# A delta-rule and SwiGLU kernel: new costs, overlaps and tile-shape changes in the planner that writes its order

## The chip, the cores and the metric

The kernel runs on one core of one Trainium2 chip. The metric is the device time in microseconds: the median of three timed runs before the change is 740.26 us (738.58 to 741.01). The engines are called here as the profile calls them: PE is TensorE (PEld its weight loads), DVE is VectorE, ACT is ScalarE, POOL is GpSimd and SP is SyncE, which issues most DMAs.

## The reference

Two blocks follow each other. The first is a delta-rule attention over 768 steps, for 4 batches and 8 heads of size 48. The second is a SwiGLU feed-forward over the 3072 tokens (model 384, hidden 1536), behind an RMS norm.

```python
k_n = k / (norm(k) + 1e-6)
for t in range(S):
    y[:, :, t] = einsum('bhd,bhde->bhe', q[:, :, t], state)
    v_old = einsum('bhde,bhd->bhe', state, k_n[:, :, t])
    state = state + beta_t * einsum('bhd,bhe->bhde', k_n[:, :, t], v[:, :, t] - v_old)
x = y.transpose(0, 2, 1, 3).reshape(B * S, H * D)
xn = x / sqrt(mean(x * x) + 1e-6) * rms_g
out = (silu(xn @ w_gate) * (xn @ w_val)) @ w_out
```

## The kernel before

The 768 steps are cut into 12 chunks of 64. Inside a chunk the recurrence becomes matrix algebra for all 32 heads of the batch at once. For each chunk the kernel does these things:

- `norms` and `prep` normalize the keys, transpose them (`turn`, L489), multiply them with each other (`scores`, L512), send the products through DRAM into another layout, and solve a triangular system on DVE. The solve is a chain of 15 planned steps, each one a product (L673) and a reduction (L679). Two merges on PE (L754 and L776) put the halves of the inverse together.
- `qpart` does the transposes and scores of the queries.
- `recur` applies the state to keys and queries (`on_state`, L815), the inverse to the corrected values (L857), the masked scores to the result (L871), and updates the state (L980). It then normalizes the rows, transposes them (L948) and forms seven sums of the feed-forward's input (L966).
- `ffn` does the feed-forward of the chunk: 30 products on PE (L1116, eight matmuls each), which DVE (L1126) or ACT (L1128) takes out of PSUM, a Silu on ACT (L1132) and a product on DVE (L1133). Then `down` (L1172, L1181) does seven products with the output weights. Both are bilinear schemes that use fewer products and more sums. Chunks 0 and 1 use `ffn_plain` (L1023, L1005) instead.

The matmuls have three kinds of tile. Most use the whole array (128 rows by 128 columns). The groups at L512, L815, L857, L871 and L980 are made of 64 small matmuls of 64 rows by 64 columns. The merges use 128 rows by 32 columns, and two early transposes (L730) 32 by 32. In steady state there are seven groups of 64 rows and two merges per chunk.

The weights come as 64-bit words (two halves of a double). Eighteen tiles are converted by a chain of four DVE operations each (L408, L414, L419, L424); for the first nine the two parts are added on PE (L439 and L440).

The order of all instructions on all engines is not written by hand. `Plan.add` records each group of instructions as an operation with an engine, a duration in microseconds, its inputs and outputs, the PSUM banks that it takes and gives back, and a first priority. `Plan.run` then plans 60 times and keeps the plan with the earliest end. `forward` simulates the engines: each time it picks, among all operations whose inputs are known, the one with the earliest start, and among equal starts the one with the smallest key. `backward` goes through the plan from its end and gives each operation the latest start that it could have as its new key. Between rounds the keys are shaken a little. The best order is then emitted, and each engine works through its part of it strictly in order. Up to 70 us filler matmuls (L1262) are put into planned gaps of PE, one per 0.2 us of gap.

The durations come from constants and four linear formulas, for instance `V = lambda n: 0.13 + 0.0011 * n` for a DVE operation over n elements and `A = lambda n: 0.2 + 0.0008 * n` for ACT. A planned result is available on another engine after `op.lat` (0.15 us, 0.7 for a DMA) plus a slack (0 to 1 us by part of the program). On its own engine it is available at once.

## Time and profile before

| | |
|---|---|
| median of 3 runs | 740.26 us (738.58 to 741.01) |
| the profiled execution's own time | 739.21 us |
| its span, first to last instruction | 737.5 us |
| mean granted PE clock | 0.996 |
| PE busy | 719.1 us (97%), 10238 matmuls |
| DVE busy | 575.0 us (78%), 1144 instructions |
| ACT busy | 308.5 us (42%) |
| POOL busy | 151.2 us (20%) |
| DMA | 54.68 MB, mean 74 GB/s |

Busy time is the time in which an engine had an instruction in work. A busy PE is not PE at its peak, since matmuls are pipelined: one of 128 columns lasts 0.277 us in the records, and the next starts 0.112 us after it. To see what PE loses between two groups, one compares the starts of the groups in the timeline, not their lengths. In a timeline line the first number is the start in us, the second the length, then come engine, line, operation, output and inputs, tile shape, size and count; brackets hold the idle time before it and what ended that. In the table of stretches each line has the stretch, its length, and then the busy time of PE, PEld, DVE, ACT and POOL with the count of instructions, the granted clock, the DMA share and GB/s.

### The profile page before, as it was taken

The numbers are of one execution on the slowest core, as the hardware profiler recorded it, in microseconds if no ns is written. First come the engines' busy times: TensorE is split into PE (matmuls) and PEld (weight loads), VectorE is DVE, ScalarE is ACT, GpSimd is POOL, SyncE is SP. The second block draws the span as 40 slices with busy tenths as digits, with TensorE's granted clock in tenths as the row PEclk, the third lists the DMA queues.
The fourth block names the chain that finished last, engine by engine and source line by source line (L and its number), as shares of the span: only waits on it lengthen the run. The fifth ranks groups of instructions, "written<-read, shape, count | busy, mean of one in ns | idle before, by whom it ended". The sixth has DMA issues, their size and how long they took to land. (4 is left out here: it accounts for less than half of the span.)

```text
span 737.5 us, 23665 instructions
## 1 busy us (share of the span) xinstructions
PE 719.1 (97%) x10238; PEld 660.1 (90%) x10238; DVE 575.0 (78%) x1144; ACT 308.5 (42%) x691; POOL 151.2 (20%) x153
## 2 busy tenths in 40 slices
PE   9999998999999999999999999999999999899997
PEld 9877766877889999999999999999999999898997
DVE  4999989789997966876967856977976876877362
ACT  4535636122335336345345355345246245244241
POOL 4100303322312111413203203203031311200000
PEclk9999999999999999999999999999999999999999
DMA  7848677331350142253152162234143123040000
GB/s 162 222 74 250 151 171 203 74 57 33 67 106 16 31 81 58 45 99 61 32 107 46 24 112 49 45 66 72 34 81 72 24 51 67 3 67 7 22 2 21
DMA packets 206999, 54.68 MB, mean 74 GB/s; under 512 B 199216, under 2 KB 202288, under 8 KB 206896
## 3 DMA queue, kind: packets, MB, share of 16 engines
q1 hardware_dynamic: 201552, 52.19, 34.3%
q10 hardware_dynamic: 5344, 0.98, 0.8%
q8 instruction: 80, 1.31, 0.7%
q14 instruction: 23, 0.19, 0.1%
HBM read 40.83 MB, written 12.32 MB: 72 GB/s over the span
## 5 line engine op out<-in xcount | busy, mean ns | idle before, releaser
L1126 DVE TENSOR_TENSOR tmp<-tmp,bank 128x512 f32<-128x512 f32 x180 | 122.2, 684 | 83.4 <-PE bank L1116 67.6
L1116 PE MATMUL bank<-xf,w_in 128*128 128x128 f32 x1440 | 181.3, 277 | 0.0
L1116 PEld LDWEIGHTS bank<-xf,w_in 128*128 128x128 f32 x1440 | 169.6, 192 | 3.5 <-issue 1.4
L1116 PE MATMUL bank<-xf,more 128*128 128x128 f32 x960 | 124.2, 277 | 0.5 <-DVE tmp L1126 0.4
L1116 PEld LDWEIGHTS bank<-xf,more 128*128 128x128 f32 x960 | 114.9, 192 | 2.4 <-DVE tmp L1126 0.8
L1128 ACT COPY tmp<-bank 128x512 f32<-128x512 f32 x120 | 68.4, 587 | 76.9 <-PE bank L1116 71.1
L679 DVE TENSOR_REDUCE acc<-acc 128x30 f32<-128x90 f32 (+4 forms) x180 | 85.1, 473 | 6.2
L1132 ACT ACTIVATE tmp<-tmp 128x256 f32<-128x256 f32 x120 | 49.9, 417 | 76.2 <-DVE tmp L1126 75.8
L673 DVE TENSOR_TENSOR acc<-acc,at 128x60 f32<-128x60 f32 (+4 forms) x180 | 65.2, 362 | 5.0 <-POOL at L656 1.2
L1133 DVE TENSOR_TENSOR hf<-tmp 128x256 f32<-128x256 f32 x120 | 57.4, 488 | 14.0 <-ACT tmp L1132 13.0
L1172 PE MATMUL bank<-wo_sb,hf 128*128 128x192 f32 x360 | 64.3, 328 | 1.1 <-DVE hf L1133 1.1
L1172 PEld LDWEIGHTS bank<-wo_sb,hf 128*128 128x128 f32 x360 | 58.1, 190 | 1.7 <-DVE hf L1133 1.3
L532 POOL TENSOR_TENSOR knrm<-ksum,half 128x16 f32<-128x16 f32 x12 | 36.7, 3060 | 105.0 <-DVE ksum L531 105.0
L626 POOL TENSOR_TENSOR at<-at,beta_b 128x1024 f32<-128x1024 f32 x10 | 24.0, 2397 | 161.4 <-DMA at<-dkk 161.4
L1262 PE MATMUL bank<-ident 128*128 128x128 f32 x310 | 38.8, 285 | 1.4 <-POOL ident masks.py:199 1.4
L1262 PEld LDWEIGHTS bank<-ident 128*128 128x128 f32 x310 | 37.3, 200 | 2.1 <-POOL ident masks.py:199 1.4
L700 POOL COPY acc<-acc 128x128 f32<-128x128 f32 x40 | 16.2, 437 | 105.4 <-DVE acc L679 104.7
L1023 PE MATMUL bank<-xp,w_in 128*128 128x256 f32 x144 | 35.0, 396 | 0.0
L1005 PE MATMUL bank<-wo_sb,hf 128*128 128x384 f32 x96 | 34.4, 491 | 0.1
L1023 PE MATMUL bank<-xf,w_in 128*128 128x256 f32 x144 | 33.6, 383 | 0.2 <-ACT xf L951 0.2
L1023 PEld LDWEIGHTS bank<-xp,w_in 128*128 128x128 f32 x144 | 28.0, 198 | 5.0
L1023 PEld LDWEIGHTS bank<-xf,w_in 128*128 128x128 f32 x144 | 26.8, 190 | 5.0 <-ACT xf L951 0.3
(172 smaller groups left out, 1079.4 us busy)
## 6 DMA issues: line engine op xcount, KB each, us to landing
at<-dkk SPq DMA_DIRECT2D x23, 256.0 KB, 4.0
more<-in_moe_w_gate_dram SPq DMA_DIRECT2D x6, 768.0 KB, 7.0
q<-in_q_dram SPq DMA_DIRECT2D x24, 192.0 KB, 4.4
more<-in_moe_w_val_dram SPq DMA_DIRECT2D x6, 768.0 KB, 7.9
vt<-in_v_dram SPq DMA_DIRECT2D x24, 192.0 KB, 3.7
more<-in_moe_w_out_dram SPq DMA_DIRECT2D x6, 768.0 KB, 5.9
out_dram<-tmp SPq DMA_DIRECT2D x48, 96.0 KB, 2.2
k<-in_k_dram SPq DMA_DIRECT2D x23, 192.0 KB, 4.1
```

Source lines behind the costliest of these rows:

```text
L532: P.add("POOL", 2.95, lambda: nc.gpsimd.tensor_tensor(out=knrm[i2], in0=ksum[i2], in1=half, op=ALU.pow), pn, r=[("ksum", i2), "half"], w=[ ...
L673: nc.vector.tensor_tensor(out=acc[:, 1:3, 0:n, j + 2 : W].rearrange("p a i t -> p i a t"), in0=acc[:, old, 0:n, j : j + 2, None].to_broadc ...
L679: nc.vector.tensor_reduce(out=acc[:, new, 0:n, j + 2 : W], in_=acc[:, lo : lo + 3, 0:n, j + 2 : W].rearrange("p a i t -> p i t a"), axis=A ...
L1005: nc.tensor.matmul(po[p].t[:, 0:DM], hf[:, spot(f), 128 * p : 128 * p + 128], wo_sb[:, spot(f)], start=(f == f0), stop=(f == f1 - 1), skip ...
L1023: nc.tensor.matmul(ps.t[:, TOK * side : TOK * side + TOK], w_in[:, side, h_, 3 * t + i_, n : n + 128], x_[:, 2 * t : 2 * t + 2].rearrange( ...
L1116: nc.tensor.matmul(g.t[:, 128 * z : 128 * z + 128], fac[:, side, 128 * f : 128 * f + 128], xf[:, xs], start=(begin and z == 0), stop=False ...
L1126: P.add("DVE", V(512), lambda t=t, g=g: nc.vector.tensor_tensor(out=t, in0=t, in1=g.t, op=ALU.add), -1, r=[g], w=[tk], last=g)
L1128: P.add("ACT", A(512), lambda t=t, g=g: nc.scalar.copy(t, g.t), -1, r=[g], w=[tk], last=g)
L1132: P.add("ACT", A(256), lambda t=t: nc.scalar.activation(out=t[:, 0:256], in_=t[:, 0:256], func=ACTF.Silu), -1, w=[tk])
L1133: P.add("DVE", V(256), lambda t=t, f0=f0, p=p: nc.vector.tensor_tensor(out=hf[:, spot(f0) : spot(f0) + 2, 128 * p : 128 * p + 128], in0=t[ ...
L1172: nc.tensor.matmul(g.t[:, 0:192], a_[:, f], b_[:, f], start=(begin and f == 0), stop=(f == 5), skip_group_check=True)
L1262: nc.tensor.matmul(warm[:, 0:128], ident, ident)
```

## The change

Only the planner's costs change; the operations themselves, their data and their banks stay as they are. There are four parts.

1. Overlap. `OVERLAP` lets an engine start its next operation 0.08 us (DVE), 0.1 us (ACT) or 0.06 us (POOL) before the last one ends, whether or not the next one uses the last one's result. The backward pass does the same.
2. Hops. `Op.hop` replaces the constant 0.15 us between engines: 0.2 us behind PE, 0.15 us from another engine to PE, 0.05 us between the others. DMAs keep their 0.7 us.
3. Tile shape. Each PE operation carries a `mode`: 64 for the groups of 64 rows, 32 for the two merges, 128 for all others (the early transposes at L730 and the small product at L593 too). When the mode differs from that of the last PE operation, the forward pass adds 0.1 us. In the choice among operations with equal start, the key of an operation whose mode differs is made worse by `STICK`, 2 us.
4. Durations. Groups of 64 rows, transposes, merges and a few others get shorter durations.

```diff
+OVERLAP = {"PE": 0.0, "ACT": 0.1, "DVE": 0.08, "POOL": 0.06, "SP": 0.0}
+STICK = 2.0
...
+    def hop(self, user):
+        return self.lat if self.dma else 0.2 if self.eng == "PE" else 0.15 if user.eng == "PE" else 0.05
...
+        op.mode = self.rows if eng == "PE" else None
...
-                    if best is None or (s, op.key, op.n) < best[0]:
-                        best = ((s, op.key, op.n), op)
+                    key = op.key + (STICK if op.mode is not None and op.mode != mode else 0.0)
+                    if best is None or (s, key, op.n) < best[0]:
+                        best = ((s, key, op.n), op)
...
-            end = at[op.eng] = s + op.dur
+            if op.mode is not None and op.mode != mode:
+                s += 0.1
+                op.start, mode = s, op.mode
+            end = s + op.dur
+            at[op.eng] = end - min(OVERLAP[op.eng], op.dur)
...
-                u.at = max(u.at, end + (0.0 if u.eng == op.eng and not op.dma else op.lat + u.slack))
+                u.at = max(u.at, at[op.eng] if u.eng == op.eng and not op.dma else end + op.hop(u) + u.slack)
...
-            op.key = front[op.eng] = t - op.dur
+            op.key = t - op.dur
+            front[op.eng] = op.key + min(OVERLAP[op.eng], op.dur)
...
-                gap = d.end - d.start - d.dur + (0.0 if d.eng == op.eng and not d.dma else d.lat + op.slack)
+                gap = d.end - d.start - d.dur + (0.0 if d.eng == op.eng and not d.dma else d.hop(op) + op.slack)
...
-                    P.add("PE", 1.5, s6, pr, r=cvk + [("cvw", n), "ident"], w=[("cvp", n, x_)], ps=ps)
+                    P.add("PE", 1.35, s6, pr, r=cvk + [("cvw", n), "ident"], w=[("cvp", n, x_)], ps=ps)
...
-            P.add("PE", 0.55, tr, pr, r=r + ["ident"], w=[ps, keys[hv]], ps=ps)
+            P.add("PE", 0.44, tr, pr, r=r + ["ident"], w=[ps, keys[hv]], ps=ps)
...
-        P.add("PE", 1.16, sc, pr, r=r, w=ps + w, ps=ps)
+        P.rows = 64
+        P.add("PE", 0.99, sc, pr, r=r, w=ps + w, ps=ps)
+        P.rows = 128
```

The other durations change in the same way, with `P.rows` around those of small tiles: merge L754 from 0.7 to 0.5 and L776 from 1.1 to 0.9 (rows 32), `on_state` from 1.1 to 0.98, L857 and L871 from 0.6 to 0.49 for each half, L980 from 1.2 to 0.98 (rows 64), the transposes at L948 from 0.45 to 0.34, the Square on ACT of chunk 0 from `A(192) + 0.2` to `A(192) + 0.15`, and `down`'s products from 1.96 to 1.95.

## The prediction, made before the changed kernel was run

> **What bounds the kernel now.** I read the page's span and busy lines first, then busy time by stretch, then TensorE's timeline.
>
> ```profile
> span 737.5 us, 23665 instructions
> ...
> PE 719.1 (97%) x10238; PEld 660.1 (90%) x10238; DVE 575.0 (78%) x1144; ACT 308.5 (42%) x691; POOL 151.2 (20%) x153
> ```
>
> TensorE has work at hand for 719.1 of 737.5 us; 18.4 us are idle. The stretches (length, then PE, PEld, DVE, ACT, POOL busy, clock, DMA) say where:
>
> ```profile
> 80.00:105.00 25.00, 23.34 (x375) 18.43 (x374) 23.85 (x45) 10.40 (x25) 4.57 (x2) 1.00 0.54 121
> 105.00:130.00 25.00, 22.62 (x526) 17.54 (x523) 22.59 (x35) 15.68 (x30) 7.13 (x4) 0.96 0.79 209
> ...
> 346.00:401.00 55.00, 53.48 (x840) 51.18 (x839) 41.83 (x92) 23.85 (x56) 13.13 (x13) 1.00 0.35 62
> ...
> 621.00:673.00 52.00, 49.47 (x753) 47.39 (x751) 39.86 (x83) 18.97 (x44) 9.35 (x11) 1.00 0.18 33
> ...
> 700.00:737.50 37.50, 32.86 (x254) 32.27 (x252) 18.17 (x35) 9.98 (x23) 0.00 (x0) 0.97 0.05 11
> ```
>
> Up to 105 us VectorE is nearly full (18.5, 18.8, 19.1 of 20 us in the stretches of 20 to 80 us, 23.85 of 25 here): the start is VectorE's, and TensorE idles 2.5 us there (0 to 80) besides fillers. From 80 to 130 it idles 1.66 + 2.38 us, from 130 to 700 the stretches add up to 7.25 us, and 4.64 us lie behind 700. So a new order can win TensorE's waits, an earlier start, or the work that TensorE does twice: changes of its tile shape. TensorE's timeline shows these (start, length, shape, count):
>
> ```profile
> 267.34 1.95 PE L1116 MATMUL bank<-xf,more 128*128 128x128 f32 x16
> 269.13 0.60 PE L489 MATMUL bank<-ident,k 128*128 128x128 f32 x4
> 269.57 1.06 PE L1116 MATMUL bank<-xf,more 128*128 128x128 f32 x8
> ...
> 407.36 1.16 PE L1116 MATMUL bank<-xf,more 128*128 128x128 f32 x8
> 408.36 1.06 PE L1116 MATMUL bank<-xf,w_in 128*128 128x128 f32 x8
> 409.34 1.15 PE L871 MATMUL bank<-u,pt 64*64 64x48 f32 x64
> 410.31 1.15 PE L512 MATMUL bank<-qt,kt 64*64 64x64 f32 x64
> 411.39 2.22 PE L1172 MATMUL bank<-wo_sb,hf 128*128 128x192 f32 x12
> ```
>
> Sixteen matmuls between other 128-row work take 269.13 - 267.34 = 1.79 us; between two 64-row groups they take 409.34 - 407.36 = 1.98, 0.19 more. A 64-row group followed by another takes 410.31 - 409.34 = 0.97; followed by 128 rows, 411.39 - 410.31 = 1.08, 0.11 more. An excursion to 64 rows and back therefore costs 0.19 + 0.11 = 0.30 us. Counting shapes along TensorE's records: 183 changes, 65 excursions to 64 rows (some 84 planned groups, so about 20 already share one), 27 to 32 columns or rows. All excursions cost about 92 x 0.30 = 28 us.
>
> **The change, part by part.** No instruction but TensorE's filler matmuls (one per 0.2 us of planned idle before 70 us; 310 now) changes in number and no byte moves; the queues of SP, ScalarE and POOL hold the same issues, in an order that the planner writes anew. Costs are constants of the planner, so each edit acts only through the order.
>
> *Tile rows (mode, +0.1 us, STICK 2.0).* Among operations that can start at the same time a 64-row group now joins the last one if its key is up to 2 us later, and a 64-row group is put off until it is 2 us more urgent than 128-row work. That needs equal start times, which a full TensorE gives. Reading before's order by hand: some 10 pairs of 64-row groups stand within 2 us of each other with neither feeding the other (114 to 119 us, 213 and 216, 294 and 297, 426 and 428, 461 to 465, 569 to 571, 574 to 576), and some 17 within 4 us, which delaying the first and advancing the second spans. Chain members (the groups at L857, then L871 and L980, which need its result copied) cannot join. Bounds: none merges, 0; every chunk from 180 us on has three excursions instead of five or six, 30 fewer, -9 us. I take 15 at 0.30: **-4.5 us**, nearest to the 17 pairs. Delaying a 64-row group by 2 us delays what queues behind it on ScalarE or VectorE (the copy of u, r, the state); the recurrence of a chunk takes some 10 to 25 us of a 55 us period (L857 begins at 402.2 and 453.8 us), so I cost it at nothing; without that slack it costs 2 us a chunk.
>
> *Durations.* A transpose group drops from 0.55 to 0.44, x transposes 0.45 to 0.34, 64-row groups 1.1 to 1.2 down to 0.98 plus the change. The timeline has 0.97 and 4 transposes in 0.44 (269.13 to 269.57). Over a steady chunk the transposes, 64-row groups and merges were planned at 4 x 0.55 + 2 x 0.45 + 2 x 1.16 + 2 x 1.1 + 3 x 1.2 + 0.7 + 1.1 = 13.0 us and become 12.2 with 5.3 excursions at 0.2 and the merges' own; by the rows above they take 12.8, since an excursion costs 0.30. The 30 products, 0.9 planned, take 0.89. So the plan was about 0.5 us a chunk too long and becomes about 0.4 too short. Nothing moves by itself: 0.
>
> *Hops.* All were 0.15; now 0.2 behind TensorE, 0.15 into it, 0.05 otherwise.
>
> ```profile
> 719.84 1.05 PE L1116 MATMUL bank<-xf,w_in 128*128 128x128 f32 x8
> ...
> 720.93 0.69 DVE L1126 TENSOR_TENSOR tmp<-tmp,bank 128x512 f32<-128x512 f32 x1 [1.21 <-PE bank L1116]
> 721.65 0.42 ACT L1132 ACTIVATE tmp<-tmp 128x256 f32<-128x256 f32 x1 [1.30 <-DVE tmp L1126]
> ```
>
> Planned end 719.84 + 0.9 = 720.74, next start 720.93: 0.19. VectorE to ScalarE: 721.65 - 721.62 = 0.03. So hops become right; where they were long, VectorE merely idled in the plan.
>
> *Overlaps.* VectorE's next operation may now start 0.08 before the last ends, whatever they are. Rows that carry the doubt (VectorE and TensorE, 637 to 643 us):
>
> ```profile
> 637.21 0.35 DVE L673 TENSOR_TENSOR acc<-acc,at 128x192 f32<-128x192 f32 x1
> 637.59 0.48 DVE L679 TENSOR_REDUCE acc<-acc 128x96 f32<-128x288 f32 x1
> ...
> 641.23 0.42 DVE L673 TENSOR_TENSOR acc<-acc,at 128x256 f32<-128x256 f32 x1
> ...
> 642.20 0.34 DVE L1181 TENSOR_TENSOR tmp<-tmp,bank 128x192 f32<-128x192 f32 x1
> ...
> 642.59 2.22 PE L1172 MATMUL bank<-wsum,hf 128*128 128x192 f32 x12 [1.45 <-DVE tmp L1181]
> ```
>
> Inside a step of the triangular solve the second instruction starts 0.03 after the first (637.59 against 637.21 + 0.35). Four steps take 641.23 - 637.21 = 4.02 us; by 0.36 + 0.0052 n m with n m of 96, 110, 120, 126 the old plan had 3.79, the new one, less 4 x 0.08, has 3.47. The short price grows from 0.06 to 0.14 us a step. Five such steps stand before L1181, and TensorE waits 1.45 us for it. Independent neighbours do overlap: over VectorE's records the gap behind an eviction is -0.08, so 18 evictions and 12 products (L1133) a chunk were each planned that much too long and become right. The old plan's errors cancelled in part; the new one keeps the short ones alone.
>
> [...]
>
> For the 7.25 us of waits between 130 and 700: lower bound all go, -7.25; upper bound, the 105 steps that follow directly on another are each 0.08 later and TensorE waits for all of it, +8.4. VectorE is idle a fifth of the time, which takes up most lateness, and the evictions' price gets better while the steps' gets worse: I take **+0.5**, nearest to no change.
>
> *80 to 130 us.* 1.94 us idle before 127.0 is followed by 24 matmuls in 7.0 us that take 0.216 x 24 = 5.2 elsewhere (clock 0.96 in that stretch). A new order need not repeat this pair: bounds -5.9 (4.04 idle and 1.85 of clock) and +4 (another such pair); I take **-1.0**, since the pair is one accident of the order; where it goes, VectorE, busy 22.6 to 23.9 of 25 us here, is late next.
>
> *Before 80 us.* VectorE is the limit and its work is unchanged. Weight conversion chains four dependent operations, each planned 0.08 short where the records have +0.03: 0.46 per tile, nine tiles, 4.1 us late against the plan at worst; at best TensorE's 2.5 idle goes. I take 0. The tail (4.64 us) is the last sums and stores: 0, at most 0.7 either way.
>
> Sum: -4.5 + 0.5 - 1.0 = -5.0 against the profiled execution's 739.21 us (737.5 of span and 1.7 around it): 734.2. That run lies 1.05 below the median 740.26, so the median should be about **735**.
>
> **Rivals.**
> *Slower, by the chained steps.* The solve's steps, planned 0.14 short, push VectorE behind and TensorE waits at L1181 and at evictions. For: the 1.45 us wait stands exactly there. Against: VectorE is idle a fifth of the time. Price: +8.4, with only five merges -1.5: 739.2 + 6.9 + 1.05 = 747. It decides once more than two thirds of 8.4 us reach TensorE (5.5 us, what the forecast gains).
> *Much faster.* Excursions fall to three a chunk (-9) and half the waits go (-3.6): 740.3 - 12.6 = 728. For: TensorE is full, so every tie counts. Against: the chain of a chunk keeps its groups apart.
> *No effect on the order that matters.* Merges stay few and waits swap places: 739 to 741. For: 20 groups share an excursion already.
>
> **How the numbers follow.** Forecast 38%, slower 28%, much faster 17%, no effect 17%. The measurement tells 0.3% (2.2 us) from no change. Faster: nearly all of the forecast, all of "much faster" and a little of "no effect", 0.55; same 0.19; slower 0.26. The range runs from 724 (both large gains and some of the start) to 748; the forecast alone spans 731 to 739.
>
> **What would show it.** Right: about 50 excursions to 64 rows instead of 65, in pairs taking 0.97 each; PE busy shortfall from 130 to 700 us near 7; the clock at 1.00 in 105 to 130. Wrong: long waits of L1172 or L1116 for VectorE behind runs of L673 and L679; first L1023 matmul (81.7 us now) later; unchanged excursions.

## The result, and the profile after

The changed kernel is slower: 748.50 us median (748.47 to 750.48, 4 runs) beside 739.42 (736.16 to 741.01, 4 runs) for the kernel before on the same chip, a ratio of 1.0135 [1.0095, 1.0175]. (A ratio, here and below, compares all runs of two kernels, with its 95% interval in brackets; it is not the quotient of the two medians.) Its profiled execution took 750.48 us. The forecast was 735, so sign and size are wrong, and the time lies just above the upper end of the range, 748. Times are medians; one execution of a later experiment, 755.84 us at a clock of 0.989, was disturbed and is left out of its median.

The page of the changed kernel, span and busy time by engine:

```profile
span 748.8 us, 23665 instructions
...
PE 723.8 (97%) x10264; PEld 667.4 (89%) x10264; DVE 557.3 (74%) x1144; ACT 310.5 (41%) x691; POOL 150.3 (20%) x153
```

The work is the same but for 26 more filler matmuls (10264 against 10238). Line numbers move by 17 to 33 in the code of the phases: the products are now L1149, their evictions L1159, `down` L1205 and L1214, the scores L529, `on_state` L838, the key transposes L506, `ffn_plain` L1056, the solve L692 and L698. Its stretches (length, then busy time of PE, PEld, DVE, ACT, POOL, clock, DMA):

```profile
80.00:105.00 25.00, 25.00 (x321) 19.12 (x323) 22.82 (x41) 15.23 (x32) 4.76 (x2) 1.00 0.71 152
105.00:130.00 25.00, 22.16 (x574) 16.73 (x567) 22.27 (x36) 11.48 (x23) 5.04 (x4) 1.00 0.92 233
130.00:200.00 70.00, 65.41 (x564) 51.02 (x557) 63.42 (x110) 18.29 (x42) 20.69 (x17) 0.95 0.23 39
200.00:346.00 146.00, 143.11 (x2158) 132.80 (x2157) 105.42 (x230) 62.46 (x143) 35.73 (x38) 1.00 0.39 72
346.00:401.00 55.00, 53.23 (x844) 51.66 (x845) 39.16 (x89) 25.30 (x57) 12.87 (x13) 1.00 0.35 62
401.00:621.00 220.00, 217.50 (x3433) 211.08 (x3435) 165.04 (x365) 100.07 (x229) 53.41 (x52) 0.99 0.32 58
...
700.00:748.80 48.80, 44.15 (x346) 43.55 (x344) 22.16 (x40) 13.27 (x29) 0.00 (x0) 0.99 0.07 17
```

From 130 to 700 us TensorE now idles 4.59 + 2.89 + 1.77 + 2.50 = 11.75 us (the two stretches left out are full), where it idled 7.25, and 130 to 200 has a clock of 0.95. The tail is as it was (4.65 idle against 4.64).

Stretches at equal times hide what is late, so the traces were also read for the time at which TensorE had done an equal share of its matmuls (each weighted by its row's start-to-start time, fillers left out). Against before, the changed kernel is 6.6 us late at 6% of the work (88.8 against 82.3 us), 9.4 at 12% (138.9 against 129.5), up to 18.3 in between (at 70%), and 11.3 at the end. In the tables below, "start" is the time to 12% and "rest" the time from there to the last matmul: before 129.5 and 603.5, after 138.9 and 605.4. Most of the loss is the start, and the rest gained nothing. Each start and rest is that of one execution, and these two stem from a series in which the kernel before had a median of 739.42 us, beside 734.49 to 736.12 in the later ones, so 2 or 3 us between rows of different series say little.

**The shape changes went as priced.** Changes of tile shape along TensorE fall from 183 to 158, excursions to 64 rows from 65 to 54. A merged pair, from the timeline of the changed kernel:

```profile
408.47 1.15 PE L1011 MATMUL bank<-u,k 64*64 64x48 f32 x64
409.44 1.11 PE L898 MATMUL bank<-u,pt 64*64 64x48 f32 x64
410.48 2.94 PE L1149 MATMUL bank<-xf,w_in 128*128 128x128 f32 x24
```

The first of the pair takes 0.97 to the next start, the second 1.04. At half of the prediction's 0.30 for each change, 25 fewer are worth 3.75 us; this is an estimate, and no run measures it by itself.

**The start is late from the first instruction.** VectorE's first instructions, before:

```profile
0.86 0.07 DVE L349 MEMSET half<- 128x16 f32 x1 [0.86 <-PEq L1280]
...
1.00 0.55 DVE L335 MEMSET k<- 128x256 f32 x2
```

and after:

```profile
7.62 0.95 DVE L548 TENSOR_REDUCE ksum<-r 128x16 f32<-128x768 f32 x1 [7.62 <-ACT r L547]
...
8.82 0.27 DVE L352 MEMSET k<- 128x256 f32 x1
```

The padding of the first keys is written behind a reduction that waits 7.62 us for a DMA and a Square. TensorE's first key transposes need that padding, and more fillers stand before them as well (70 instead of 42). Before:

```profile
1.41 6.71 PE L1262 MATMUL bank<-ident 128*128 128x128 f32 x42 [1.41 <-POOL ident masks.py:199]
7.96 1.04 PE L489 MATMUL bank<-ident,k 128*128 128x128 f32 x8
```

and after:

```profile
1.42 10.75 PE L1295 MATMUL bank<-ident 128*128 128x128 f32 x70 [1.42 <-POOL ident masks.py:199]
12.00 1.04 PE L506 MATMUL bank<-ident,k 128*128 128x128 f32 x8
```

They start at 12.00 us instead of 7.96, the solve's first scaling (L645) at 32.36 instead of 27.95 behind 2.37 us of waiting for a DMA, and the first feed-forward matmul at 85.91 instead of 81.72. In this plan the 4 us do not come back.

**TensorE stalls inside groups, and the profile names no releaser.** TensorE's waits from 130 us on ("issue" is a wait behind which nothing shows; in us in total, times, longest), the longest ones before:

```profile
PE bank L1172 <- DVE tmp L1181: 2.9, 3, 1.5
PE bank L512 <- issue: 1.1, 2, 0.7
...
PE bank L815 <- issue: 0.5, 1, 0.5
```

and after:

```profile
PE bank L838 <- issue: 4.6, 2, 3.0
PE bank L529 <- issue: 3.1, 2, 1.7
PE bank L884 <- issue: 1.5, 1, 1.5
PE bank L1149 <- DVE tmp L1159: 1.4, 2, 1.0
...
PE bank L1205 <- DVE tmp L1214: 0.4, 1, 0.4
```

Waits for VectorE fell from 5.8 to 2.1 us, but waits for nothing rose from 1.6 to 9.2. All but one of these (1.5 us in front of a single group, L884 at 186.04 us) lie in the middle of 64-row groups that follow each other, as here in TensorE's timeline:

```profile
124.75 1.03 PE L529 MATMUL bank<-qt,kt 64*64 64x64 f32 x52
128.08 0.39 PE L529 MATMUL bank<-qt,kt 64*64 64x64 f32 x11 [2.30 <-issue]
...
129.24 0.93 PE L838 MATMUL bank<-state,kt 64*64 64x48 f32 x49
133.18 0.57 PE L838 MATMUL bank<-state,kt 64*64 64x48 f32 x12 [3.02 <-issue]
...
135.15 1.85 PE L506 MATMUL bank<-ident,q 128*128 128x128 f32 x8
```

Three groups lose 5.3 us, and eight transposes behind them take 1.85 us that take 1.04 at 12.00: the trace records a granted clock of 0.50 from 133.34 us on, for 3.41 us.

So there were three suspects: how the planner chooses (the start), what the merged groups run into (the stalls), and the price of chained steps, which the prediction had named as the danger.

### The profile page after: what moved, and what is told of

The parts are those of the page before. It is cut to its first block, busy times and chain, and to the rows that moved or that the text cites. A ratio compares the mean times of both kernels' runs of the same rounds, so it can differ in the third digit from the quotient of the medians.

```text
span 748.8 us, 23665 instructions
## 1 busy us (share of the span) xinstructions
PE 723.8 (97%) x10264; PEld 667.4 (89%) x10264; DVE 557.3 (74%) x1144; ACT 310.5 (41%) x691; POOL 150.3 (20%) x153
## 3 DMA queue, kind: packets, MB, share of 16 engines
q8 instruction: 80, 1.31, 0.8%
## 4 chain that ended last, share of the span: by engine, by line
PE 77%; DVE 13%; issue 3%; SPq 3%; DMA 2%; ACT 1%; POOL 1%; DVEq 0%; POOLq 0%; ACTq 0%
PE bank L1149 30%; PE bank L1205 17%; PE bank L1056 8%; PE bank L1038 3%; DVE acc L698 3%; PE bank L529 3%; SPq L340 3%; DVE acc L692 3%; PE bank L838 2%; PE bank L506 2%; PE bank L1295 2%; DVE tmp L1159 2%; DMA at<-dkk 2%; PE bank L884 1%; PE bank L797 1%
## 5 line engine op out<-in xcount | busy, mean ns | idle before, releaser
L1149 PE MATMUL bank<-xf,w_in 128*128 128x128 f32 x1440 | 182.7, 278 | 0.2
L1159 DVE TENSOR_TENSOR tmp<-tmp,bank 128x512 f32<-128x512 f32 x180 | 120.7, 681 | 73.9 <-PE bank L1149 69.7
L1149 PEld LDWEIGHTS bank<-xf,w_in 128*128 128x128 f32 x1440 | 170.8, 192 | 3.1 <-DVE tmp L1159 0.6
L1149 PE MATMUL bank<-xf,more 128*128 128x128 f32 x960 | 125.1, 277 | 1.4 <-DVE tmp L1159 1.4
L1149 PEld LDWEIGHTS bank<-xf,more 128*128 128x128 f32 x960 | 115.7, 192 | 3.8 <-DVE tmp L1159 2.0
L698 DVE TENSOR_REDUCE acc<-acc 128x30 f32<-128x90 f32 (+4 forms) x180 | 85.1, 473 | 6.2
L692 DVE TENSOR_TENSOR acc<-acc,at 128x60 f32<-128x60 f32 (+4 forms) x180 | 63.4, 352 | 3.3
L1205 PE MATMUL bank<-wo_sb,hf 128*128 128x192 f32 x360 | 63.7, 327 | 0.3 <-DVE xp L1198 0.3
L1205 PEld LDWEIGHTS bank<-wo_sb,hf 128*128 128x128 f32 x360 | 58.2, 190 | 0.6 <-ACT kk L626 0.4
L645 POOL TENSOR_TENSOR at<-at,beta_b 128x1024 f32<-128x1024 f32 x10 | 23.8, 2384 | 173.0 <-DMA at<-dkk 132.9
L1166 DVE TENSOR_TENSOR hf<-tmp 128x256 f32<-128x256 f32 x120 | 52.7, 452 | 7.5 <-ACT tmp L1165 6.9
L1214 DVE TENSOR_TENSOR tmp<-tmp,bank 128x192 f32<-128x192 f32 x30 | 10.6, 353 | 46.5 <-PE bank L1205 39.6
L1295 PE MATMUL bank<-ident 128*128 128x128 f32 x336 | 42.4, 288 | 1.4 <-POOL ident masks.py:199 1.4
L1295 PEld LDWEIGHTS bank<-ident 128*128 128x128 f32 x336 | 41.0, 203 | 2.2 <-POOL ident masks.py:199 1.4
L1038 PE MATMUL bank<-wo_sb,hf 128*128 128x384 f32 x96 | 36.5, 511 | 0.0
L1056 PE MATMUL bank<-xf,w_in 128*128 128x256 f32 x144 | 34.3, 384 | 0.0
L1056 PE MATMUL bank<-xp,w_in 128*128 128x256 f32 x144 | 32.9, 380 | 0.1
L719 POOL COPY acc<-acc 128x128 f32<-128x128 f32 x40 | 19.9, 528 | 64.6 <-DVE acc L698 64.3
L1056 PEld LDWEIGHTS bank<-xp,w_in 128*128 128x128 f32 x144 | 27.0, 190 | 5.4 <-ACT qt L518 0.4
```

The lines of the kernel that those rows point to most:

```text
L692: nc.vector.tensor_tensor(out=acc[:, 1:3, 0:n, j + 2 : W].rearrange("p a i t -> p i a t"), in0=acc[:, old, 0:n, j : j + 2, None].to_broadc ...
L698: nc.vector.tensor_reduce(out=acc[:, new, 0:n, j + 2 : W], in_=acc[:, lo : lo + 3, 0:n, j + 2 : W].rearrange("p a i t -> p i t a"), axis=A ...
L1038: nc.tensor.matmul(po[p].t[:, 0:DM], hf[:, spot(f), 128 * p : 128 * p + 128], wo_sb[:, spot(f)], start=(f == f0), stop=(f == f1 - 1), skip ...
L1056: nc.tensor.matmul(ps.t[:, TOK * side : TOK * side + TOK], w_in[:, side, h_, 3 * t + i_, n : n + 128], x_[:, 2 * t : 2 * t + 2].rearrange( ...
L1149: nc.tensor.matmul(g.t[:, 128 * z : 128 * z + 128], fac[:, side, 128 * f : 128 * f + 128], xf[:, xs], start=(begin and z == 0), stop=False ...
L1159: P.add("DVE", V(512), lambda t=t, g=g: nc.vector.tensor_tensor(out=t, in0=t, in1=g.t, op=ALU.add), -1, r=[g], w=[tk], last=g)
```

## The experiments

All ratios are against the kernel before on the same chip. "Seed" is the seed with which the planner shakes its due times: another seed gives another order by the same rules, and so shows how much one plan's luck is worth.

### A probe of TensorE's instruction supply

This is a small program of its own, with runs of 1, 1, 2, 3, 4 and 6 groups of 64 small matmuls (48 columns), six groups with 192 columns, and one more, parted by 80 matmuls of the whole array. The series runs twice, the second time beside loads of 192 KB. These loads end at 182 us, and the program's own store of 4.6 MB follows them until 194 us: so the second run of four stands beside the store, and the second run of six beside nothing.

> This kernel leaves the whole computation out: it runs groups of 64 small TensorE matmuls (64 by 64 tiles) in runs of 1, 1, 2, 3, 4, 6 groups between stretches of 128-row matmuls, once more 6 groups with 192 instead of 48 moving columns, then 1; first with no other transfers, then the whole series again beside 48 loads of 192 KB. Theory 'instruction supply': a 64-row group holds 128 instructions in 0.97 us, and TensorE's own instruction transfers of 16 KB (256 instructions) cannot follow two or three groups in a row. Then runs of 1 pass at 0.97 to 1.08 us, runs of 4 and 6 with 48 columns show gaps of 1 us or more inside a group that the profile puts down to nothing it shows, the run of 6 with 192 columns (same number of instructions, several times longer) shows none, and the gaps grow in the second series. Rival 'tile shape': the gaps come with every group of 64 rows, and also with 192 columns. Rival 'something of the kernel' (PSUM banks, data not shown): no gaps here at all.

TensorE's timeline, the quiet series (runs of 3, 4 and 6, and the 192 columns):

```profile
51.38 3.01 PE L39 MATMUL ps<-mov,ident 64*64 64x48 f32 x192
...
63.45 3.35 PE L39 MATMUL ps<-mov,ident 64*64 64x48 f32 x211
67.99 0.90 PE L39 MATMUL ps<-mov,ident 64*64 64x48 f32 x45 [1.19 <-issue]
...
83.63 2.07 PE L39 MATMUL ps<-mov,ident 64*64 64x48 f32 x125 [1.63 <-issue]
...
96.05 15.83 PE L39 MATMUL ps<-mov,ident 64*64 64x192 f32 x384
```

and the second series (the run of 3 beside the loads, that of 4 beside the store, and the end of that of 6):

```profile
172.12 0.32 PE L39 MATMUL ps<-mov,ident 64*64 64x48 f32 x5 [1.96 <-issue]
...
188.58 2.59 PE L39 MATMUL ps<-mov,ident 64*64 64x48 f32 x85 [4.33 <-issue]
191.10 10.88 PE L31 MATMUL warm<-ident 128*128 128x128 f32 x80
...
210.14 0.79 PE L39 MATMUL ps<-mov,ident 64*64 64x48 f32 x37 [1.65 <-issue]
210.86 10.83 PE L31 MATMUL warm<-ident 128*128 128x128 f32 x80
```

Nothing in this program depends on another engine, and three groups in a row run without a stall in quiet; four lose 1.19 us. Beside the loads three lose 1.96 us, and beside the store four lose 4.33, after which 80 matmuls take 10.88 us instead of the 9.20 that they take between the other runs. The form with 192 columns has the same tiles and as many instructions, takes 15.83 us for six groups in both series, 2.7 times as long as six at 0.97, and shows no stall. So in these runs neither the tile shape nor the number of instructions makes the stalls, but how fast the instructions follow each other: 128 in 0.97 us against 128 in 2.64. The page's queue "q8 instruction" moves 80 packets with 1.31 MB in the kernel, 16 KB each, while TensorE has 2 x 10264 instructions (a matmul and its weight load each): 257 instructions a packet. Their number goes with TensorE's instructions: 35 packets in the probe with its 4492 matmuls, 81 in e3_port_chain with 10334. By this count, an estimate, two 64-row groups need a packet in 1.94 us. While the quiet run of six stalled, the packets started at 81.21, 84.72 and 88.47 us, one in 3.5 to 3.8. So the author's reading is that the instructions run short there; why shorter runs pass is not shown. How much of the longer stalls of the second series is due to the transfers is not shown either: the runs also fall on other places in a packet there.

The kernel's own stalls stand beside these packets in time. In the 20 traces (the probe's among them) TensorE has 71 waits of over 0.4 us behind which nothing shows, from 20 us on; 69 of them end 1.2 to 1.75 us after a packet has landed, while the packets come 8.9 us apart on average. In the changed kernel packets land at 126.43 and 131.74 us, and the two stalls shown above end at 128.08 and 133.18. In the kernel before one lands at 125.47, and the idle 1.94 us end at 127.01. The two exceptions are L884 in the changed kernel (1.50 us) and a merge in the run with `STICK = 0.0` (1.28 us). A wait that ends so behind a packet is called an instruction stall below.

### The port edit: how the start got lost

The planner holds that DVE and POOL share a port (no run tests that), and lets one use it only after the other's end. The change lets POOL itself come free 0.06 us before its end, but holds the port until the end. POOL's next memset could then always start 0.06 us before VectorE's, and the earliest start wins whatever the urgency. Before, both starts were equal, and the key decided.

```diff
             if op.port:
-                held[op.eng] = end
+                held[op.eng] = at[op.eng]
```

> The changed kernel, but in the planner the port that VectorE and GpSimd share is given back 0.06 or 0.08 us before an operation's end, as the engine itself is. Theory 'port': GpSimd's overlap of 0.06 lets its next memset always start before VectorE may, so VectorE's memsets of the keys' padding are planned behind all six of GpSimd's, at 5.3 us, the first transposes are planned at 7.1 instead of 4.3 us, and 28 more filler matmuls hold TensorE until 12.0 us instead of 8.0. Here the first transposes begin at 8 us and the time falls by 4, to 744. Rival 'the start is paid elsewhere': the transposes begin at 8 us, but the first feed-forward matmul still begins 3 us or more later than in the kernel before, because the plan counts chained VectorE operations too short: 747 to 749.

Measured: 735.36 us, ratio 0.9995 [0.9973, 1.0016]. TensorE's first key transposes, behind 44 fillers instead of 70:

```profile
9.32 1.04 PE L506 MATMUL bank<-ident,k 128*128 128x128 f32 x8
```

The transposes start at 9.32 instead of 12.00, the first feed-forward matmul at 77.73 instead of 85.91, and the start takes 128.0 us. So the rival, by which that first matmul still comes 3 us late, falls. With one line of the planner changed, this plan has lost nothing against the kernel before. It also has 5.2 us of instruction stalls instead of 12.2, and no half clock instead of 10.24 us of it; how much of the gain is the port is taken up below, with the other seeds.

### Taking the overlap or the preference away

```diff
-OVERLAP = {"PE": 0.0, "ACT": 0.1, "DVE": 0.08, "POOL": 0.06, "SP": 0.0}
+OVERLAP = {"PE": 0.0, "ACT": 0.0, "DVE": 0.0, "POOL": 0.0, "SP": 0.0}
```

> The changed kernel with all overlaps set to 0; durations, hops and the price of tile shapes stay. Theory 'overlaps': the loss of 11 us comes from VectorE being planned too short, at the start and after. Then the first feed-forward matmul begins within 1 us of the kernel before (81.7 us), and with the shape changes saved the time is 735 to 738. Rival 'instruction supply' alone: the start is mended (-6), but adjacent groups of 64 rows still stall TensorE by some 14 us against 5 before: 741 to 744. Rival 'luck of the plan': 745 to 750.

Measured: 744.92 us, ratio 1.0102 [1.0053, 1.0151]. The transposes come at 8.46 us, so the overlap is what unbalanced the port; but the start is still 132.7 us and the rest 607.1. The sign of the theory, a first feed-forward matmul within 1 us of 81.7, is missed: it comes at 86.86. The overlap alone is not the whole loss. This plan has 6.7 us of instruction stalls and 6.83 us of half clock, against 4.0 and 3.41 in the kernel before.

```diff
-STICK = 2.0
+STICK = 0.0
```

> The changed kernel with STICK 0: a change of tile shape still costs 0.1 us in the plan, but nothing is put off to join groups of 64 rows. Theory 'instruction supply': adjacent groups become few again, TensorE's waits put down to nothing the profile shows fall from 14 to 5 us or less, the clock stays full, and against 3 us of shape changes that come back the time falls by 5 to 8, to 741 to 744. Rival 'the merges are a gain': the time rises by 3, to 752. The start stays as late as in the changed kernel in both.

Measured: 744.77 us, ratio 1.0125 [1.0075, 1.0174]. Shape changes go up to 193 and stalls without a releaser after 130 us go down to 1.6 us. Start 131.2 (expected as late as with the preference, 138.9), rest 606.9. Without the preference the rest is within 1.5 us of the change with it: about 35 more changes cost 5.2 us, and 3.8 us fewer waits (8.2 against 12.0) give most of it back. In this planner the preference bought nothing: what it saves in shape changes it pays in instruction stalls.

### Other seeds: how much is luck

```diff
-        rng = random.Random(1)
+        rng = random.Random(2)
```

(or 3), for the change as it is, for the change with the port edit, and for the kernel before.

> The changed kernel with another start of the planner's random shaking (2 instead of 1), to see how much of a time is the luck of one plan. Theory 'port': the memsets are again planned behind GpSimd's, the first key transposes begin at 11 us or later, and the time is 744 to 752. Rival 'luck of the plan': the time may land anywhere from 733 to 752, and the pair with the port mended overlaps with it.

> The same with start 3. Theory 'port': 744 to 752, first key transposes at 11 us or later. Rival 'luck of the plan': anywhere from 733 to 752. Theory 'instruction supply': its waits on nothing the profile shows grow with the number of places where three 64-row groups stand in a row (7 planned here, 8 in the changed kernel, 4 with start 2).

> The port mended as in e1_port, start 2. Theory 'port': first key transposes before 9.5 us, 733 to 739. Rival 'luck of the plan': e1_port was a lucky plan, and this one lies at 740 to 750. Theory 'instruction supply': this plan has seven runs of three and two of five 64-row groups, more than the changed kernel, so the waits on nothing shown are 10 us or more and the time is at the upper end, 738 or above.

> The port mended, start 3. Theory 'port': first key transposes before 9.5 us, 733 to 739. Rival 'luck of the plan': 740 to 750. Theory 'instruction supply': three runs of three groups and one of five, so 4 to 6 us of such waits.

> The kernel before with another start of the planner's shaking (2). It tells how much of the gap of 5 us that is left between the changed kernel with the port mended (735, 744, 743) and the kernel before is the luck of the old plan. Theory 'the rest is luck': 738 to 746. Rival 'the rest is the new costs' (overlaps for chained operations): 733 to 738.

> The same with start 3. Theory 'the rest is luck': 738 to 746; rival 'the rest is the new costs': 733 to 738. This plan has two runs of four 64-row groups and two of three, so theory 'instruction supply' expects 4 to 8 us of waits on nothing shown.

| planner | seed | ratio | start | rest | waits after 130 us: for DVE, for nothing shown | instruction stalls from 20 us on, time at half clock before the program's last 12 us |
|---|---|---|---|---|---|---|
| before | 1 | 1 | 129.5 | 603.5 | 5.8, 1.6 | 4.0, 3.41 |
| before | 2 | 0.9954 [0.9935, 0.9973] | 126.8 | 600.5 | 3.5, 0.6 | 3.4, 0 |
| before | 3 | 1.0013 [0.9989, 1.0036] | 123.0 | 605.1 | 7.6, 1.2 | 1.3, 3.41 |
| after | 1 | 1.0135 [1.0095, 1.0175] | 138.9 | 605.4 | 2.1, 9.2 | 12.2, 10.24 |
| after | 2 | 1.0133 [1.0095, 1.0171] | 132.8 | 608.1 | 7.2, 2.7 | 5.9, 3.41 |
| after | 3 | 1.0185 [1.0152, 1.0217] | 135.9 | 607.6 | 8.1, 3.3 | 5.7, 6.83 |
| port edit | 1 | 0.9995 [0.9973, 1.0016] | 128.0 | 603.2 | 4.5, 4.6 | 5.2, 0 |
| port edit | 2 | 1.0109 [1.0077, 1.0140] | 130.5 | 606.2 | 8.4, 1.7 | 2.9, 6.83 |
| port edit | 3 | 1.0110 [1.0065, 1.0155] | 127.2 | 608.2 | 12.1, 1.4 | 2.3, 0 |

The loss of the change is no luck: its three plans average 1.0151, those of before 0.9989. The whole recovery of e1_port was partly luck: its three average 1.0071. So the plans with the port edit have 0.8% of the 1.6% less, nearly all in the start (135.9 to 128.6 on average, the rest 607.0 to 605.9).

That is not all the port's. In all three seeds the transposes come 2.5 to 2.7 us earlier with the edit (9.32, 8.91 and 9.12 against 12.00, 11.39 and 11.80), and 6% of TensorE's work is done some 2.8 us earlier on average, about half of the 5.8 us by which the change is behind the kernel before there. The first feed-forward matmul shows it less clearly: 85.91, 80.98 and 82.84 in the change, 81.72, 80.75 and 79.72 before. But the plans with the edit have fewer instruction stalls too. Stalls and half of the time at half clock, an estimate of what both cost, come to 11.3 us a plan in the change, 4.6 with the edit and 4.0 before. This difference, 6.7 us, is as large as the whole recovery, and no run tells whether the edit or chance makes it. By this estimate stalls and clock are some 7 of the 12 us that the change loses.

The 9.2 us of stalls belong to one plan, but the two others wait for VectorE in their place, and the waits of all three are 11 to 12.5 us together with ScalarE's, against 4.1 to 8.8 before. With the port edit TensorE still waits 4.5 to 12.1 us for VectorE. So another cause lies in the rest.

The length of the runs alone does not foretell the stalls. Counted from the planned runs of three groups and more, 10 us or more of waits for nothing shown were expected with the port edit and seed 2, 4 to 6 with seed 3, and 4 to 8 in the kernel before with seed 3. They were 1.7, 1.4 and 1.2.

### Chained steps at their own price

In the records of the kernel before, the product and reduction of a solve step, of which the second uses the first's result, stand 0.03 us apart in all 180 places, while the median gap of VectorE behind an eviction (L1126) is -0.08 us (130 places where the next instruction follows within 0.2 us). The change's forward pass gives both the second price. (Its backward pass does not: there only operations that do not use each other's result overlap, since `gap` is 0 on the same engine.) On top of the port edit, and on all engines:

```diff
-                u.at = max(u.at, at[op.eng] if u.eng == op.eng and not op.dma else ...
+                u.at = max(u.at, end + 0.03 if u.eng == op.eng and not op.dma else ...
```

> The changed kernel with the port mended and with the overlap taken from operations that use the last one's result on the same engine (their start is the end plus 0.03, as the trace has it); independent ones keep it. Theory 'chained steps': the plan no longer runs ahead of VectorE at the start and in the solve, TensorE's waits for VectorE fall, and the time is 730 to 736. Rival 'luck of the plan': 735 to 744 as the three plans with the port mended alone.

Measured: 741.28 us, ratio 1.0092 [1.0059, 1.0126], so the 730 to 736 us of the theory are missed, and the rival's 735 to 744 hold it. The rest falls to 597.9 us, below all nine plans above, and the waits for VectorE to 2.2. But the start takes 139.7, with the first feed-forward matmul at 93.45 us. VectorE's timeline shows why:

```profile
36.00 0.26 DVE L692 TENSOR_TENSOR acc<-acc,at 128x112 f32<-128x112 f32 x1
36.30 0.35 DVE L698 TENSOR_REDUCE acc<-acc 128x56 f32<-128x168 f32 x1
36.56 0.55 DVE L425 TENSOR_SCALAR w_in<-w_in 128x768 uint32<-128x768 uint32 x1
37.02 0.31 DVE L692 TENSOR_TENSOR acc<-acc,at 128x156 f32<-128x156 f32 x1
37.37 0.42 DVE L698 TENSOR_REDUCE acc<-acc 128x78 f32<-128x234 f32 x1
37.72 0.95 DVE L431 SCALAR_TENSOR_TENSOR w_in<-more,w_in 128x768 uint32<-128x768 uint32 x1
38.58 0.35 DVE L692 TENSOR_TENSOR acc<-acc,at 128x192 f32<-128x192 f32 x1
```

Between two steps of the first solve a weight conversion slips in (L425, L431). From the first reduction to the end of the last this solve takes 18.3 us, and 13.0 in the kernel before. A conversion whose inputs are there can start 0.11 us before the next step, so it goes ahead, however little urgent: the fault of the port again, in another place.

A variant also lets the third 64-row group in a row rank behind 128-row work (`row_` counts the groups of one run):

```diff
-                    key = op.key + (STICK if op.mode is not None and op.mode != mode else 0.0)
+                    key = op.key + (STICK if op.mode is not None and (op.mode != mode if row_ < 2 else op.mode == 64) else 0.0)
```

> As e3_port_chain, and behind two 64-row groups a third is made less urgent instead of more. Theory 'instruction supply': no waits of over 0.7 us inside 64-row groups, 1 to 3 us less than e3_port_chain: 729 to 734. Rival 'supply is hidden or rare': the same as e3_port_chain within 2 us.

Measured: 741.24 us, ratio 1.0092 [1.0055, 1.0128]; start 141.4 with the solve at 18.4 us, rest 594.2, stalls without a releaser 0.7 against 1.2. The cap moves the total by nothing that can be told. It does show that the late start is not one of stalls: this start has 1.7 us of them and no half clock, against 4.8 and 3.41 us in the run above, and is as late.

### A window, so that urgency decides again

On each engine the most urgent operation among those that can start within 0.15 us of the earliest is taken. This covers both 0.06 and 0.11. The port edit and the price of chained steps stay:

```diff
             for e in ENGINES:
+                mine = []
                 for op in cand[e]:
...
-                    if best is None or (s, key, op.n) < best[0]:
-                        best = ((s, key, op.n), op)
+                    mine.append((s, key, op.n, op))
+                if mine:
+                    edge = min(mine)[0] + 0.15
+                    s, key, n, op = min((m for m in mine if m[0] <= edge), key=lambda m: (m[1], m[0], m[2]))
+                    if best is None or (s, key, n) < best[0]:
+                        best = ((s, key, n), op)
```

> The changed kernel with three edits to its planner: the shared port held only until the engine comes free, a dependent instruction of the same engine starting 0.03 us after the end of the one before, and, new, a window of 0.15 us: on each engine the most urgent of the instructions that can start within 0.15 us of that engine's earliest is taken, instead of the earliest whatever its urgency. The shape preference and the 0.1 us for a shape change stay. Theory 'tie-breaking' (the late start of e3_port_chain is the same fault as the one that its port edit mended: a plan that always takes the earliest start lets a piece of work that is free 0.1 us sooner go ahead of the next step of an urgent chain): the start comes back, the first FFN product of the queue work (L1023 in before) at 76 to 83 us instead of 93.45, the steady part keeps what e3_port_chain had (597.9 us from 12% of TensorE's work to the end, waits for VectorE and for nothing shown after 130 us at most 4.5 us together), sum 724 to 731 us, ratio 0.983 to 0.995. Rival 'the true price of the chain costs the start by itself' (the start of this program is bounded by VectorE's chain, and pricing it rightly only uncovers that): first FFN product at 90 us or later and 738 to 743 us, ratio 1.005 to 1.012.

> e4_window with another seed of the planner's shaking of due times (2 instead of 1). 'Tie-breaking': within 4 us of e4_window, 723 to 733 us, so that the gain belongs to the edits and not to one lucky plan. 'Chance of one plan': more than 6 us away from e4_window, on the other side of the kernel before.

> e4_window with seed 3. 'Tie-breaking' as the cause: 726 to 735 us, ratio 0.988 to 1.000, so that the three plans of it average some 731 us, against 748.0 for the three plans of the change as it is; a late start again (12% of TensorE's work done after 133 us) would say that the window mends one plan by chance.

Two variants of it: the window and the port edit, with the chained steps left as the change has them; and all three edits with `STICK = 0.0`.

> The changed kernel with the port edit and the window of 0.15 us, but with the planned overlap of dependent VectorE, ScalarE and GpSimd steps left as the change has it. If the overlap of dependent steps is worth the 6 us or so that separated the steady parts of e1_port and its seeds (603 to 608 us) from e3_port_chain (598): start as in e4_window, PE's waits after 130 us 8 us or more, 731 to 738 us, ratio 0.995 to 1.004, that is 4 to 10 us above e4_window. If the overlap costs nothing once urgency decides: within 2 us of e4_window.

> e4_window without the preference for instructions of the same tile shape (STICK 0), the 0.1 us price of a shape change left in place. It plans 184 runs of one shape instead of 166, so 9 excursions more. If merging shape changes is worth what the trace prices it at, 0.30 us for each excursion: 2 to 4 us above e4_window. If runs of adjacent 64-row groups give it back in stalls that show nothing: equal to e4_window or below it, with fewer of those stalls. If due times put back by the preference cost more than both: 3 us or more below e4_window.

> e4_window_no_preference with seed 2, to stand beside e4_window_seed2 (0.9949) as e4_window_no_preference (1.0002) stood beside e4_window (0.9899). If the preference for the same tile shape is worth 3 us or more in a plan that is otherwise sound: ratio 0.999 to 1.006, with more waits of TensorE for VectorE than the 1.6 us of e4_window_seed2 after 130 us and 5 to 9 excursions more. If the 7 us between the first two were the luck of one plan: ratio 0.990 to 0.997.

| planner | seed | us | ratio | shape changes | start | rest | waits of TensorE after 130 us |
|---|---|---|---|---|---|---|---|
| window | 1 | 729.20 | 0.9899 [0.9856, 0.9941] | 173 | 127.8 | 595.6 | 2.9 |
| window | 2 | 731.68 | 0.9949 [0.9926, 0.9973] | 174 | 131.4 | 593.8 | 1.6 |
| window | 3 | 729.47 | 0.9916 [0.9885, 0.9946] | 166 | 128.3 | 597.1 | 4.0 |
| chained steps too short | 1 | 741.15 | 1.0063 [1.0031, 1.0095] | 165 | 136.3 | 599.5 | 7.8 |
| no preference | 1 | 736.30 | 1.0002 [0.9985, 1.0020] | 192 | 128.6 | 603.8 | 6.4 |
| no preference | 2 | 737.65 | 1.0034 [1.0014, 1.0055] | 193 | 125.7 | 603.5 | 4.9 |

The page and TensorE's waits of e4_window, the latter from 130 us on:

```profile
span 727.8 us, 23703 instructions
...
PE 717.7 (99%) x10268; PEld 663.1 (91%) x10268; DVE 566.5 (78%) x1144; ACT 308.6 (42%) x691; POOL 154.9 (21%) x153
```

```profile
PE bank L1210 <- DVE state L1025: 1.5, 1, 1.5
PE bank L903 <- DVE u L928: 0.6, 1, 0.6
```

and VectorE's timeline at the end of the first solve (L697 and L703 are its step, L430 a conversion):

```profile
49.22 0.22 DVE L697 TENSOR_TENSOR acc<-acc,at 128x60 f32<-128x60 f32 x1
49.47 0.28 DVE L703 TENSOR_REDUCE acc<-acc 128x30 f32<-128x90 f32 x1
49.67 0.55 DVE L430 TENSOR_SCALAR w_in<-w_in 128x768 uint32<-128x768 uint32 x1
```

The solve runs through in 13.0 us, the conversions follow it, and the kernel is faster than the kernel before and than the change: the three plans average 0.9921, against 0.9989 and 1.0151. With seed 3 the first solve takes 14.1 us. The rival, that the true price of the chain costs the start by itself, falls: with the same price the start is 127.8 instead of 139.7. One number of the expectation missed: the first feed-forward matmul came at 84.67, not by 83 us. The start as a whole is no better than before's (123.0 to 129.5); the gain is in the rest (593.8 to 597.1 against 600.5 to 605.1).

With the chained steps left too short this planner is 12 us slower, more than the 731 to 738 us expected, and not only where expected: its waits are 7.8 us, and its start 136.3, with stalls of 2.34 and 2.75 us inside runs of 64-row groups that end at 77.11 and 132.28. Only one seed of this was run. It has 5.6 us of instruction stalls and 10.24 us of half clock, and e4_window has neither; by the estimate above that is 10.7 of the 12 us, so what the price of chained steps is worth beside the window is not shown. The other two window plans have 3.5 and 1.3 us of stalls and 3.41 us of half clock each.

The preference for the same shape is now worth 7.1 us (seed 1) and 6.0 (seed 2), more than the 2 to 4 expected: about 20 shape changes at 0.15 are 3 us, and the waits are 3.4 us fewer (6.4 against 2.9, 4.9 against 1.6). Those are two different plans, so what moves the waits is not shown. The plans without the preference are no faster than the kernel before, so this planner gains only with it. The window with the old costs was not run.

## Why the prediction was wrong, by its own steps

The terms against the profiled execution, with the late time at equal work:

| term | predicted | bounds | measured |
|---|---|---|---|
| before 80 us | 0 | -2.5 to +4.1 | +6.6 (to 6% of the work) |
| 80 to 130 us | -1.0 | -5.9 to +4 | +2.8 (6 to 12%) |
| merged shapes and waits after that, tail | -4.0 | -16.9 to +9.1 | +1.9 |
| sum | -5.0 | | +11.3 |

*"VectorE is the limit and its work is unchanged ... I take 0."* This step failed, and in the profiled plan its bound too. I bounded it with the lateness of chained conversions; the cause that the runs show is no price but a choice. The edit that lets an engine come free early does not do so for the port that the planner has it share, and a planner that prefers the earliest start then orders work by 0.06 us instead of by urgency. At 6% of the work the three plans of the change are 5.8 us late on average, and the port edit gives back some 2.8 of it; what makes the other half is open. The code was in the prediction's hands: it says of the preference that it "needs equal start times", and did not ask which ties the overlap breaks.

*"Delaying a 64-row group ... I cost it at nothing."* Failed. I looked for the work that queues behind a delayed group, and not for stalls inside two or three groups in a row. In the profiled plan instruction stalls rose from 4.0 to 12.2 us and the time at half clock from 3.41 to 10.24, which takes back more than the 3.75 us that the merged shapes gain by the prediction's price (11 excursions fewer instead of 15). Over three plans stalls and clock cost some 11.3 us instead of 4.0, the largest part of the loss.

*80 to 130 us: "A new order need not repeat this pair."* It repeated it: the idle 1.94 us with the half clock behind it, seen before at 125 to 127 us, became 5.3 us at 125.7 to 133.2. I took it for an accident of the order; it is an instruction stall behind 64-row groups close together, and the change puts more of them side by side (7 pairs and 5 runs of three before, 14 and 7 after). Not every new order repeats it: e1_port has no stall of over 0.5 us there. The sign named for it, the clock at 1.00 in 105 to 130 us, came true only because the slow stretch moved to 130 to 200 (0.95).

*Waits from 130 to 700 us: +0.5.* They are 11.75 instead of 7.25, that is +4.5, within the bounds, but in the profiled plan not from chained steps: waits for VectorE fell to 2.1 us. The sign named for the slower rival, long waits of `down` behind the solve, is not there (0.4 us). So that rival's time, 747, was near the truth by another mechanism. Chained steps do cost time all the same: with them at their own price the rest falls to 594 to 598 us, in all five plans that keep the preference. The prediction saw this fault in the rows, with the right sizes. For waits on VectorE alone its +0.5 was about right: they average 5.8 us in the three plans of the change and 5.6 before. But it took before's errors to make up for the fault, and the three plans with the port edit wait 8.3 us on average.

*Signs.* About 50 excursions: 54 (of 82 groups of 64 rows in the records, where the prediction reckoned 84). First feed-forward matmul later, named as a sign of being wrong: it is, by 4.2 us.

That neighbours overlap and chained steps do not, as the prediction read it from its rows, shows in the rows of e3_port_chain above too: the conversion at 36.56 starts 0.09 us before the reduction ahead of it ends, while a chained reduction starts 0.04 after its product (36.30). In these rows what decides is whether the next operation uses the last one's result.

What stays open: the new hops and the shorter durations were not run by themselves. The change without overlap is still at 1.0102, and which of them, or the preference with its stalls, makes that is not settled. Nor is it settled how many of the instruction stalls an edit causes and how many are the luck of a plan.

## What to carry to other kernels

In a planner that takes the earliest start and asks for urgency only between equal starts, every refinement of a cost by some hundredths of a microsecond decides order. Let urgency decide within a window wider than the overlaps before the costs are refined: here the same costs gave 1.0092 without the window and 0.9899 with it (seed 1; two other seeds with it gave 0.9949 and 0.9916). And count instructions, not only matmul time, where small matmuls are put side by side: in the probe, three groups of 128 instructions in a row lost 1.96 us beside loads, and four lost 1.19 us in quiet.

## What the runs showed of the hardware that was not expected

- TensorE stalls inside some runs of 64-row groups, 128 instructions in 0.97 us each: in the probe 1.19 us were lost in a run of four groups in quiet, 1.96 in a run of three beside loads and 4.33 in a run of four beside a store. Six groups with 192 columns in the same form, as many instructions in 15.83 us, lost nothing. The profile names no releaser for such a stall. The instruction queue of the page moves packets of 16 KB (80 in the kernel), and 69 of 71 waits of this kind end 1.2 to 1.75 us after one of them has landed.
- Half clock is recorded beside some of these stalls and not beside others. In the probe the granted clock is 0.79 over 186 to 202 us, around the stall of 4.33 us that ends at 188.58, and 0.91 over 202 to 221 us, where 1.04 and 1.65 us were lost with 2.08 us of work between them (the 80 matmuls behind them take 10.83 us instead of 9.20). Behind 1.63 and 1.13 us, with 2.07 us of groups and 0.60 us of whole-array matmuls between, 77 matmuls take 8.76 us, as fast as elsewhere; neither of these two had loads or stores beside it. In the kernel before, half clock is recorded from 128.01 us on, for 3.41 us, behind 1.94 us of idle that end at 127.01. What decides between these cases is not shown.
